# A three-stage kernel on one core: the short key step moved inside its chunk, the second sample's low-rank sums moved beside the channel mixer

## The chip, the cores and the metric

The program runs on one core of a Trainium2 chip. Its engines work side by side, each through a list of its own in program order: TensorE (PE) multiplies, and its weight loads (PEld) overlap the products; VectorE (DVE) and ScalarE (ACT) work element by element; GpSimd (POOL) does little here but issue DMAs; SyncE (SP) issues most DMAs. Semaphores order work between engines. The metric is the device time of one execution in microseconds (us).

## The reference

Batch 2, sequence S = 3136, width 256, key width 64. Three stages, each fed by the one before, in fp32:

```
attention:  a = max(z z^T / S, 0)^2            scores S x S, key width 64
            x = u * (a v)
layer 1:    h = (x^T U) V  (rank 32 over the sequence);  y = x + h^T
            out1 = y + max(y w1a, 0) w2a       256 -> 1024 -> 256
layer 2:    m = real(fft2(out1));  y = out1 + m
            n = (y - mean) / sqrt(var + 1e-6)  over the width
            out2 = y + max(n w1b, 0) w2b
```

## The kernel before

All large products use numbers split into a high part (rounded to the matmul's format, fp32r) and a low part (the rest); a product is high x high + high x low + low x high. The split costs one cast and one subtraction an operand (`hcopy` on ACT, `sub` on DVE, lines 92 to 96; profile rows with L93 and L96 are all of these).

*Attention* (lines 380 to 691). Per sample there are 7 chunks of 448 queries, 14 in all. A chunk runs over 13 key steps `p`: steps 0 to 11 take 256 keys. The key width of 64 fills half of the array's rows, so its two halves hold two blocks of keys, and two matmuls run side by side as a pair. `scores` (line 521) issues 6 matmuls (3 pairs), then ACT takes max and square (L541, L544), and DVE casts (L545) and subtracts. `values` and `products` (lines 552 to 587) multiply with the values into four PSUM banks, two per half `a` of the width: 12 pairs for a full step. Step 12 holds only the 64 keys that are left: 3 half-wide score pairs and 3 product pairs. It is the last of its chunk; the `a = 1` half of step 11 is put behind the `a = 0` half of step 12. Then `gate` (line 589) adds the two banks of each half and multiplies by u on DVE and stores the result to DRAM (`aT_d`) on SP. The scores run two steps ahead of the products (`LAG = 2`); at the last step of a chunk (`turn`) they come after the gate instead of before the products. PSUM has two double banks for scores and the four for sums.

Beside the steps, `ahead` and the main loop issue loads and splits: keys (`load_z`, `split_z`), queries, values (`load_v`, `split_v`; those of the second sample in chunk 6), and `conversions`: 41 generators that turn U, V and the four weight matrices from 64-bit words into high and low parts, one started every second step from step 9 on, at most two at once, each advanced once a step but for the last two steps of a chunk.

*Passage and layer 1.* When the attention's pools are closed, new ones take their memory: `mp` for working tiles, `xpool` for the attention's result, three pools for the eight PSUM banks. For each sample `mixer` (line 726) transposes 25 token tiles of 128, casts, and sums them with U into one bank, two tiles behind; `misc()` gives the transposes one of three banks in turn. For the first sample, 12 tiles come from four early loads into the common pool's P tiles, the rest from four large loads of `xT`. `finish_G` copies the sums, multiplies with a replicating matrix and splits. Then the second sample's mixer runs two tiles at a time, in turn with the first sample's `finish_G` and the first chunk's `prep1`; only when both are through, the 28 chunks of the channel mixer begin (14 of layer 1, 14 of layer 2; lines 993 to 1017), 8 steps each: `hidden` (6 matmuls), then `project` of the step before the last (6 matmuls). Generators in `active` advance once a step beside them: the next chunk's preparation, the second layer's Fourier transform (`fourier`, whose `features` ends in four DVE operations and eight additions), and its weights.

What sets the order is the program order on each engine, written out by hand by these loops. The parts that the change touches are `Weights.split` (181), `finish_G` (210), `load_z` (393), `split_v` (449), `scores` (521), `products` to `gate` (552 to 596), the loop over `steps` (598 to 691), the pools (703 to 724), `mixer` (726), `features` (867), `weights` (950) and the opening (979 to 992).

## Time and profile before

| | |
|---|---|
| median of 3 runs | 1207.67 us (1206.24 to 1208.36) |
| profiled execution, its own time | 1207.86 us |
| its span, first to last instruction | 1206.1 us |
| mean granted TensorE clock | 0.992 |
| instructions | 21307 |
| DMA moved | 69.39 MB, 58 GB/s over the span |

The time of an execution is a little longer than its span. In the rows further down, a line of a timeline is: start and length in us, engine, source line, operation, tiles written <- read, shapes, count, and in brackets how long the engine was idle before and what ended that. 9 in PE's slices of the page means 90% or more:

```profile
## 2 busy tenths in 40 slices
PE   8999999999999999997899999999999999999998
PEld 7899999898999999996799998999998888999997
DVE  7878887899778666565544646475676788767674
ACT  7877777887777666663422324333255444444442
POOL 0001000000000000000000000110000110000000
PEclk9999999999999999998999999999999999999999
```

Attention fills slices 1 to 18, layer 1 about 20 to 29.

### The profile page before, as it was taken

What the parts mean: (1) busy time and instruction counts of PE and PEld (TensorE: products, weight loads), DVE (VectorE), ACT (ScalarE), POOL (GpSimd) and SP (SyncE); (2) the same over time, 40 slices, a digit from 0 to 9 for tenths busy, and PEclk for the clock granted to TensorE, in tenths of its full rate; (3) what the DMA queues carried; (4) which work ended last, traced back from release to release, by engine and by line L of the source; (5) the groups of instructions that cost most, each with busy time, mean ns of one, the idle gap of its engine ahead of it and who ended that gap; (6) DMA issues with size and microseconds to landing.
All of it is one profiled execution on the core that took longest, in us unless ns stands there. A gap on an engine that the chain in (4) does not pass through costs nothing.

```text
span 1206.1 us, 21307 instructions
## 1 busy us (share of the span) xinstructions
PE 1180.0 (98%) x8488; PEld 1080.5 (90%) x8488; DVE 831.5 (69%) x1581; ACT 662.6 (55%) x1102; POOL 52.7 (4%) x104
## 2 busy tenths in 40 slices
PE   8999999999999999997899999999999999999998
PEld 7899999898999999996799998999998888999997
DVE  7878887899778666565544646475676788767674
ACT  7877777887777666663422324333255444444442
POOL 0001000000000000000000000110000110000000
PEclk9999999999999999998999999999999999999999
DMA  4303322243212111017000101211012111111111
GB/s 133 103 17 88 89 65 71 58 139 118 81 51 92 44 40 39 1 45 282 8 16 17 29 9 61 60 26 33 8 49 81 49 45 28 39 31 39 32 39 46
DMA packets 58691, 69.39 MB, mean 58 GB/s; under 512 B 11294, under 2 KB 52672, under 8 KB 58592
## 3 DMA queue, kind: packets, MB, share of 16 engines
q1 hardware_dynamic: 52896, 60.72, 15.9%
q0 software_dynamic: 5696, 7.31, 3.0%
q8 instruction: 67, 1.10, 0.4%
q14 instruction: 32, 0.26, 0.1%
HBM read 47.96 MB, written 19.96 MB: 56 GB/s over the span
## 4 chain that ended last, share of the span: by engine, by line
PE 82%; DVE 9%; ACT 4%; DMA 3%; issue 2%; SPq 0%; DVEq 0%; ACTq 0%
PE psO L567 29%; PE psH L324 7%; PE psH L326 7%; PE psH L325 7%; PE psC L350 7%; PE psC L349 7%; PE psC L351 7%; PE psS L535 7%; PE psC L733 1%; DMA vraw<-in_v 1%; ACT P L544 1%; DVE Hl L330 1%; ACT P L541 1%; DVE h L545 1%; DVE Vt L96 1%
## 5 line engine op out<-in xcount | busy, mean ns | idle before, releaser
L567 PE MATMUL psO<-h,Vt 64*128 64x448 f32 x2744 | 434.7, 366 | 2.2 <-DVE aT L594 1.5
L567 PEld LDWEIGHTS psO<-h,Vt 64*128 64x128 f32 x2744 | 279.2, 185 | 24.6 <-DVE aT L594 4.9
L567 PE MATMUL psO<-l,Vt 64*128 64x448 f32 x1372 | 274.5, 368 | 1.3 <-DVE l L96 1.3
L330 DVE SCALAR_TENSOR_TENSOR Hl<-psH,Hh 128x448 fp32r<-128x448 f32 x224 | 138.9, 622 | 157.0 <-ACT Hh L329 155.8
L96 DVE TENSOR_TENSOR l<-P,h 128x896 fp32r<-128x896 f32 (+2 forms) x211 | 209.9, 995 | 24.0 <-ACT h L93 17.7
L329 ACT ACTIVATE Hh<-psH 128x448 fp32r<-128x448 f32 x224 | 120.9, 542 | 180.5 <-PE psH L326 179.4
L541 ACT ACTIVATE P<-psS 128x896 f32<-128x896 f32 (+1 forms) x183 | 161.3, 882 | 96.2 <-PE psS L535 94.8
L545 DVE CAST h<-P 128x896 fp32r<-128x896 f32 (+1 forms) x183 | 110.5, 604 | 106.6 <-ACT P L544 106.0
L544 ACT ACTIVATE P<-P 128x896 f32<-128x896 f32 (+1 forms) x183 | 168.5, 922 | 5.8
L324 PE MATMUL psH<-h,w 128*128 128x448 f32 x448 | 167.7, 374 | 0.0
L349 PE MATMUL psC<-Hh,w 128*128 128x448 f32 x448 | 163.7, 365 | 1.4 <-DVE P L372 1.4
L350 PE MATMUL psC<-Hl,w 128*128 128x448 f32 x448 | 163.7, 365 | 0.9 <-DVE Hl L330 0.9
L326 PE MATMUL psH<-h,w 128*128 128x448 f32 x448 | 164.2, 366 | 0.0
L325 PE MATMUL psH<-l,w 128*128 128x448 f32 x448 | 164.0, 366 | 0.0
L351 PE MATMUL psC<-Hh,w 128*128 128x448 f32 x448 | 163.0, 364 | 0.0
L567 PEld LDWEIGHTS psO<-l,Vt 64*128 64x128 f32 x1372 | 143.0, 185 | 13.8 <-DVE l L96 3.8
L535 PE MATMUL psS<-Q,KT 64*128 64x448 f32 x1002 | 130.5, 363 | 2.2 <-ACT KT L93 1.9
L535 PEld LDWEIGHTS psS<-Q,KT 64*128 64x128 f32 x1002 | 99.0, 185 | 8.7 <-ACT KT L93 2.4
L349 PEld LDWEIGHTS psC<-Hh,w 128*128 128x128 f32 x448 | 84.0, 188 | 9.5 <-issue 1.9
L350 PEld LDWEIGHTS psC<-Hl,w 128*128 128x128 f32 x448 | 84.1, 188 | 9.1 <-DVE Hl L330 2.1
L324 PEld LDWEIGHTS psH<-h,w 128*128 128x128 f32 x448 | 84.3, 188 | 7.6
L326 PEld LDWEIGHTS psH<-h,w 128*128 128x128 f32 x448 | 84.1, 188 | 7.5
(282 smaller groups left out, 1159.4 us busy)
## 6 DMA issues: line engine op xcount, KB each, us to landing
uT<-in_uT SPq DMA_DIRECT2D x14, 448.0 KB, 4.4
aTd<-aT SPq DMA_DIRECT2D x14, 448.0 KB, 2.9
vraw<-in_v SPq DMA_DIRECT2D x24, 256.0 KB, 2.8
out<-P SPq DMA_DIRECT2D x27, 224.0 KB, 2.0
scr<-wst SPq DMA_DIRECT2D x16, 256.0 KB, 2.0
xT<-aTd SPq DMA_DIRECT2D x2, 1600.0 KB, 8.4
Vs<-Vd POOLq DMA_DIRECT2D x28, 112.0 KB, 2.5
rs<-rsd POOLq DMA_DIRECT2D x14, 224.0 KB, 3.6
```

The source lines that it names most:

```text
L96: tt(out=o, in0=a, in1=b, op=ALU.subtract)
L324: mm(ps[:, 0:CH], wh, self.h[:, a], start=a == 0, stop=False)
L325: mm(ps[:, 0:CH], wh, self.l[:, a], start=False, stop=False)
L326: mm(ps[:, 0:CH], wl, self.h[:, a], start=False, stop=a == 1)
L330: stt(out=l, in0=ps[:, 0:CH], scalar=0.0, in1=f(h), op0=ALU.max, op1=ALU.subtract)
L349: mm(dst, wh, h, start=k == 0, stop=False)
L350: mm(dst, wh, l, start=False, stop=False)
L351: mm(dst, wl, h, start=False, stop=k == 7)
L535: mm(ps[:, j, 0:w], k, q[r, kq, o : o + w], start=(kk, kq) == (0, 0), stop=kq == 1)
L541: act(out=dst, in_=ps[:, j : j + m, 0:w], func=AF.Relu, scale=1.0 / S)
L544: act(out=A[:, x], in_=A[:, x], func=AF.Square)
L567: mm(o[fa][i][:, 0:CH], vt[r, j, k, fa * 128 : fa * 128 + 128], x[r, j * CH : j * CH + CH], start=p == 0 and n == 0, stop=p == 12 and (a = ...
```

## The change

- The order of key steps becomes 0 to 5, 12, 6 to 11: the short step is the seventh of its chunk, the gate comes after step 11, and the held-back half is that of step 10. Key loads follow the new order.
- `scores` multiplies high x high, then key high x query low, then key low x query high.
- At the start, the first keys are loaded from ACT's queue, the first value tile is cast on DVE, and the first scores are issued ahead of the loop.
- Conversions start every third step instead of every second, from step 13 on, and none in the first sample's first and last chunk.
- The last chunk's gate works in a P tile of the common pool and stores on POOL's queue; three early loads (9 tiles) follow instead of four.
- The PSUM pools of the mixer stage are opened in another order; `xT` comes in seven pieces in the order of use.
- The first sample's 25 tiles run alone; then `finish_G` and the first chunk's preparation run beside 12 tiles of the second sample; its other 13 tiles, one a step, and its `finish_G` run beside the channel mixer's first steps. `finish_G` yields twice, and the clearing of its tile comes first.
- A yield splits `features` after its four DVE operations, and the cast and subtraction of the second layer's weights fall into two steps; one more buffer for them.

```diff
@@ -180,6 +180,10 @@
...
+            for _ in self.parts(k, y):
+                pass
+
+        def parts(self, k, y):
             part, q = divmod(k, 2)
...
@@ -190,6 +194,7 @@
...
             hcopy(dst[:, 0], y)
+            yield
             sub(dst[:, 1], y, f(dst[:, 0]))
...
@@ -208,8 +213,8 @@
     def finish_G(b, g, P):
-        nc.vector.memset(P[64:128], 0.0)
         nc.vector.tensor_copy(P[0:64], g[0:64, 0:D])
+        yield
         yield
...
@@ -396,7 +401,8 @@
...
                     src = zT[b, :, i * 768 : i * 768 + 768].rearrange("d (p j n) -> d j p n", j=2, n=128)
-                    load(out=raw[r], in_=src[:, j])
+                    dma = nc.scalar.dma_start if (b, i) == (0, 0) else load
+                    dma(out=raw[r], in_=src[:, j])
                 else:
...
@@ -449,7 +455,7 @@
...
             t = Vt[b, p] = big.tile([128, 2, 2, D], F32R, tag="V", name="Vt", bufs=13)
-            hcopy(t[:, 0:n, 0, :], raw[:, 0:n, :])
+            (nc.vector.tensor_copy if (b, p) == (0, 0) else hcopy)(t[:, 0:n, 0, :], raw[:, 0:n, :])
             sub(t[:, 0:n, 1, :], raw[:, 0:n, :], f(t[:, 0:n, 0, :]))
@@ -523,7 +529,7 @@
...
             w = CH if p < 12 else CH // 2
-            for kk, kq in ((0, 0), (1, 0), (0, 1)):
+            for kk, kq in ((0, 0), (0, 1), (1, 0)):
                 for j, r in enumerate(halves):
...
@@ -532,7 +538,7 @@
...
                     o = j * w if p == 12 else 0
-                    mm(ps[:, j, 0:w], k, q[r, kq, o : o + w], start=(kk, kq) == (0, 0), stop=kq == 1)
+                    mm(ps[:, j, 0:w], k, q[r, kq, o : o + w], start=(kk, kq) == (0, 0), stop=kk == 1)
             A, h, l = ptile(), ctile("h", F32R), ctile("l", F32R)
...
@@ -569,7 +575,7 @@
...
                         start=p == 0 and n == 0,
-                        stop=p == 12 and (a == 1 or n + i == 1),
+                        stop=p == 11 and n == len(todo) - 1,
                     )
...
@@ -579,23 +585,26 @@
...
-            if p == 12:
-                products(b, qc, 11, 1)
-                del prob[b, qc, 11]
-            if p != 11:
+            if p == 11:
+                products(b, qc, 10, 1)
+                del prob[b, qc, 10]
+            if p != 10:
                 products(b, qc, p, 1)
...
         def gate(b, qc):
-            t = att.tile([128, 2, CH], F32, tag="aT", name="aT")
+            last = (b, qc) == (1, NC - 1)
+            t = c2(ptile()) if last else att.tile([128, 2, CH], F32, tag="aT", name="aT")
             o, u = acc.pop((b, qc)), uq.pop((b, qc))
...
             tt(out=t, in0=t, in1=u, op=ALU.mult)
-            load(out=aT_d[b][:, :, qc * CH : qc * CH + CH].rearrange("a p n -> p a n"), in_=t)
-
-        steps = [(b, qc, p) for b in range(NB) for qc in range(NC) for p in range(NP)]
+            (late_dma if last else load)(out=aT_d[b][:, :, qc * CH : qc * CH + CH].rearrange("a p n -> p a n"), in_=t)
+
+
+        order = [*range(6), 12, *range(6, 12)]
+        steps = [(b, qc, p) for b in range(NB) for qc in range(NC) for p in order]
         LAG = 2
...
@@ -613,25 +622,29 @@
...
         load_v(0, 1)
+        load_z(0, 1)
         split_q(0, 0)
-        load_z(0, 1)
         split_v(0, 0)
         split_z(0, 0)
-        started, converting = [0], []
+        scores(0, 0, 0)
+        started, converting = [10], []
...
                 b, qc, p = steps[i]
-                scores(b, qc, p)
+                if i:
+                    scores(b, qc, p)
+                p = i % NP
                 if qc == 0 and b == 0:
...
                         if p < 6:
-                            load_z(0, 2 + p // 2)
-                        split_z(0, 1 + p // 2)
+                            load_z(0, (4, 2, 3)[p // 2])
+                        split_z(0, (1, 4, 2, 3)[p // 2])
                     if p > 0:
-                        split_v(0, p)
+                        split_v(0, order[p])
                     if p + 2 < NP:
-                        load_v(0, p + 2)
+                        load_v(0, order[p + 2])
                 if p == 2:
...
@@ -642,7 +655,8 @@
...
                     active.append(constants())
-                if i >= 9 and i - started[-1] >= 2 and len([g for g in active if g in converting]) < 2:
+                quiet = (b, qc) not in ((0, 0), (0, NC - 1))
+                if quiet and i - started[-1] >= 3 and len([g for g in active if g in converting]) < 2:
                     job = next(jobs, None)
...
@@ -655,7 +669,7 @@
...
         for i in range(-LAG, len(steps)):
-            turn = i >= 0 and steps[i][2] == NP - 1
+            turn = i >= 0 and steps[i][2] == 11
             if not turn:
...
@@ -664,23 +678,24 @@
...
                     ahead(i + LAG)
+                n = i % NP
                 if b == 0 and qc == NC - 1:
                     load_v(1, p)
-                    if p > 0:
-                        split_v(1, p - 1)
+                    if n > 0:
+                        split_v(1, order[n - 1])
                 if (b, qc, p) == (1, 0, 0):
-                    split_v(1, NP - 1)
+                    split_v(1, 11)
                 if (b, qc) == (1, NC - 1):
...
                         chunks[0].load()
-                    if p == NP - 2:
-
-                        for k in range(4):
+                    if p == 11:
+
+                        for k in range(3):
                             t = ptile().rearrange("p (a n) -> p a n", a=2)[:, :, 0:384]
...
                 for g in list(active):
-                    if p >= NP - 2 and (b, qc) != (1, NC - 1):
+                    if n >= NP - 2 and (b, qc) != (1, NC - 1):
                         break
...
@@ -700,10 +715,10 @@
...
     xpool = ctx.enter_context(tc.tile_pool(name="xpool", bufs=1))
-    psH = late["psH"] = ctx.enter_context(tc.tile_pool(name="psH", bufs=3, space=PSUM))
     psX = ctx.enter_context(tc.tile_pool(name="psX", bufs=1, space=PSUM))
     psC = late["psC"] = ctx.enter_context(tc.tile_pool(name="psC", bufs=1, space=PSUM))
-    misc_pools.extend((psX, t) for t in "mxg")
+    psH = late["psH"] = ctx.enter_context(tc.tile_pool(name="psH", bufs=3, space=PSUM))
+    misc_pools.extend([(psX, "m"), (psX, "x"), (psC, "C1")])
...
@@ -719,13 +734,15 @@
...
-    for b in range(NB):
-        for s in (slice(1536, S), slice(0, 1536)):
-            load(out=xT[b][:, :, s], in_=aT_d[b][:, :, s].rearrange("a p n -> p a n"))
+    def load_x(b, s, e):
+        load(out=xT[b][:, :, s:e], in_=aT_d[b][:, :, s:e].rearrange("a p n -> p a n"))
...
-        g = psC.tile([128, 512], F32, tag=f"C{b}", name=f"psC{b}")
+        pool, tag = ((psC, "C0"), (psX, "g"))[b]
+        g = pool.tile([128, 512], F32, tag=tag, name="ps_" + tag)
+        P = mp.tile([128, 512], F32, tag="wst", name="wst")[:, 0:D]
+        nc.vector.memset(P[64:128], 0.0)
...
@@ -737,7 +754,7 @@
...
             for a in range(2):
-                if b == 0 and k < 12:
+                if b == 0 and k < 9:
                     t = early[k // 3][:, a, k % 3 * 128 : k % 3 * 128 + 128]
...
@@ -750,12 +767,11 @@
...
                 sums(*ready.pop(0))
-            if k % 2:
-                yield
+            yield
         while ready:
...
         yield
-        yield from finish_G(b, g, mp.tile([128, 512], F32, tag="wst", name="wst")[:, 0:D])
+        yield from finish_G(b, g, P)
...
@@ -888,6 +904,7 @@
...
             end = first + n // 64
+            yield
...
@@ -948,10 +965,10 @@
...
     def weights(i):
-        ts = {}
+        ts, halfway = {}, []
         for k in range(12):
             if k < 8:
-                ts[k] = mp.tile([128, 256], F32, tag="wraw", name="wraw", bufs=3)
+                ts[k] = mp.tile([128, 256], F32, tag="wraw", name="wraw", bufs=4)
                 load(out=ts[k], in_=wb_d[i][k])
...
@@ -963,9 +980,12 @@
...
                     sub(y[:, a], y[:, a], ps[:, 0:128])
-                wb[i].split(k - 2, ts.pop(k - 2))
-            elif 1 < k < 10:
-                wb[i].split(k - 2, ts.pop(k - 2))
+            for p in list(halfway):
+                next(p, None)
+                halfway.remove(p)
+            if 1 < k < 10:
+                halfway.append(wb[i].parts(k - 2, ts.pop(k - 2)))
+                next(halfway[-1])
             yield
...
@@ -976,20 +996,24 @@
...
+        for b, s, e in (
+            (0, 1152, 1792), (0, 1792, 2464), (0, 2464, S), (0, 0, CH), (1, 0, 1568), (0, CH, 1152), (1, 1568, S),
+        ):
+            load_x(b, s, e)
+        mix0, mix1 = mixer(0), mixer(1)
+        for _ in range(26):
+            next(mix0)
+
         def first():
-            yield
-            yield from last_G
+            yield from mix0
+            yield
             yield from chunks[0].prep()
-        mix0, mix1 = mixer(0), mixer(1)
-        for _ in range(13):
-            next(mix0)
-        last_G = mix0
-        opening = [mix1, first()]
-        while opening:
-            for g in list(opening):
-                if next(g, "end") == "end":
-                    opening.remove(g)
+        for _ in first():
+            next(mix1)
+            next(mix1)
+        misc_pools.pop()
+        active.append(mix1)
         for i in range(nstep + 2):
...
@@ -1015,6 +1039,8 @@
...
                     active.remove(g)
+                    if g is mix1:
+                        misc_pools.append((psX, "g"))
```

## Rows read from the trace of the kernel before

**Rows 1.** Page, busy us (share of the span) and instructions of each engine.

```profile
PE 1180.0 (98%) x8488; PEld 1080.5 (90%) x8488; DVE 831.5 (69%) x1581; ACT 662.6 (55%) x1102; POOL 52.7 (4%) x104
```

**Rows 2.** PE's wait list: waiter <- releaser: total us, times, longest us.

```profile
PE psC L733 <- ACT nh L93: 7.1, 2, 6.7
...
PE psO L567 <- DVE aT L594: 1.5, 2, 1.2
...
PE psC L349 <- DVE P L372: 1.4, 1, 1.4
```

**Rows 3.** Windows: length, busy us (instructions) per engine, PEclk, DMA share, GB/s.

```profile
551.83:562.07 10.24, 3.69 (x17) 3.42 (x17) 2.12 (x6) 2.04 (x6) 1.14 (x4) 0.51 1.01 401
...
582.55:585.97 3.42, 3.11 (x15) 3.11 (x16) 1.82 (x6) 1.20 (x4) 0.00 (x0) 0.54 0.00 0
```

**Rows 4.** Timeline of PE, score matmuls: start, us, line, operation, tiles, count, [idle before].

```profile
45.45 0.77 PE L535 MATMUL psS<-Q,KT 64*128 64x448 f32 x6
...
317.49 0.37 PE L535 MATMUL psS<-Q,KT 64*128 64x448 f32 x2
...
508.11 0.58 PE L535 MATMUL psS<-Q,KT 64*128 64x448 f32 x4
...
540.36 0.77 PE L535 MATMUL psS<-Q,KT 64*128 64x448 f32 x6
...
543.42 0.49 PE L535 MATMUL psS<-Q,KTl 64*128 64x224 f32 x6
```

**Rows 5.** Timeline, end of attention and first sums of the mixer.

```profile
549.11 0.36 PE L567 MATMUL psO<-h,Vt 64*128 64x448 f32 x1
...
550.73 1.09 DVE L595 TENSOR_TENSOR aT<-aT,uT 128x896 f32<-128x896 f32 x1
...
557.95 0.37 ACT L93 CAST nh<-ps_m 128x256 fp32r<-128x256 f32 x1 [7.91 <-DMA aTd<-aT]
...
558.38 0.47 PE L733 MATMUL psC<-nh,Uhl 128*64 128x256 f32 x1 [6.73 <-ACT nh L93]
```

**Rows 6.** Timeline, second sample's sums and the channel mixer's first matmul.

```profile
575.91 0.45 PE L215 MATMUL ps_x<-wst,repc 128*128 128x256 f32 x1 [0.57 <-DVE wst L212]
...
579.59 1.02 POOL L230 DMA_DIRECT2D Vs<-Vd  x2 [20.46 <-PE ps_x L244]
...
580.92 0.38 PE L744 MATMUL ps_m<-ident,xT 128*128 128x128 f32 x2
...
581.38 0.38 PE L744 MATMUL ps_x<-ident,xT 128*128 128x128 f32 x2
...
581.85 0.62 DVE L96 TENSOR_TENSOR l<-P,h 128x448 fp32r<-128x448 f32 x1 [0.63 <-ACT h L93]
...
592.30 0.55 PE L324 MATMUL psH<-h,w 128*128 128x448 f32 x1
```

**Rows 7.** Timeline, the start.

```profile
6.96 0.62 ACT L93 CAST Vt<-vraw 128x512 fp32r<-128x512 f32 x1 [2.54 <-DMA vraw<-in_v]
...
8.05 0.47 PE L535 MATMUL psS<-Q,KT 64*128 64x448 f32 x2 [1.85 <-ACT KT L93]
...
8.83 1.80 PE L535 MATMUL psS<-Q,KT 64*128 64x448 f32 x10 [0.31 <-DVE KT L96]
...
10.43 0.58 PE L567 MATMUL psO<-h,Vt 64*128 64x448 f32 x2
```

**Rows 8.** Timeline of DVE at the turn of a chunk.

```profile
164.56 1.09 DVE L96 TENSOR_TENSOR l<-P,h 128x896 fp32r<-128x896 f32 x1
...
165.56 0.62 DVE L594 TENSOR_TENSOR aT<-psO,aT 128x448 f32<-128x448 f32 x1
```

**Rows 9.** Page, costliest groups: count, busy us, mean ns, idle before.

```profile
L541 ACT ACTIVATE P<-psS 128x896 f32<-128x896 f32 (+1 forms) x183 | 161.3, 882 | 96.2 <-PE psS L535 94.8
...
L545 DVE CAST h<-P 128x896 fp32r<-128x896 f32 (+1 forms) x183 | 110.5, 604 | 106.6 <-ACT P L544 106.0
...
L544 ACT ACTIVATE P<-P 128x896 f32<-128x896 f32 (+1 forms) x183 | 168.5, 922 | 5.8
```

## The prediction

> **What bounds the kernel now.** I read the page's busy line first, then PE's wait list, then the timeline at each place that the list names, then windows with the granted clock. PE is busy for 98% of the span [rows 1], so removing busy time of another engine is worth nothing by itself; only PE's idle time, its waits too short to be listed, and its time at the lower clock can go. The wait list has one large entry: 7.1 us on PE for the first sums of the low-rank product [rows 2]. The rest is small: 1.5 us for the gate that ends an attention chunk, 1.4 us for a chunk's end in the second layer [rows 2]. The windows add to the passage from attention to the channel mixer two stretches, 10.24 and 3.42 us long, in which the granted clock is about 0.5, the 1.2 GHz level [rows 3].
>
> Attention hides a loss that the list does not show. A full step is 15 pairs of 448-column matmuls (3 of scores, 12 of products; the two of a pair run side by side on 64 rows each); two score starts in a row lie 543.42 - 540.36 = 3.06 us apart [rows 4], 0.204 us a pair. A chunk is 12 such steps (180 pairs), the short step's 3 product pairs, and its 3 score pairs at half width (some 0.11 each): 183 x 0.204 + 0.33 = 37.7 us. The undisturbed chunks take (508.11 - 317.49) / 5 = 38.12 us [rows 4], so 0.4 us is lost in each. All twelve from 45.45 to 508.11 take 462.66 [rows 4], 5.2 us more than 12 x 38.12: those are the chunks that also convert weights and split the second sample's values.
>
> **The change, part by part.** The sum is made against the profiled execution, 1207.86 us (span 1206.1); it stands 0.2 us above the median of 1207.67.
>
> *The first wait of the mixer.* PE's last attention product starts at 549.11; the gate's product on DVE ends at 550.73 + 1.09 = 551.82; but ACT's first cast of the mixer comes at 557.95, ended by the landing of the gate's own store [rows 5]. The cast writes memory that the attention's pools held, and the store was still reading from there. The change puts the last gate's tile into the common pool and its store on POOL's queue, so the last reader of the old memory is the DVE product. Then the cast can start at 551.85 and the first sums 558.38 - 557.95 = 0.43 us behind it, at 552.3 instead of 558.38: 6.1 us. Least: 0, if another transfer still holds that memory. Most: 6.1 plus half of the 3.69 us that PE worked at the lower clock until 562.07 [rows 3], 7.9. I take 6.1, since PE still idles some 2 us there. Late next is the data: the first sums take nine token tiles from three early loads, which no longer stand behind the gate's store on SP. The tenth needs 640 columns, 0.66 MB. At the 401 GB/s of the first stretch [rows 3] that is 1.6 us from the attention's end, about 549.5; the pieces ahead of the second sample, 2432 columns, and its own 1568 take 10.2 us, until about 560 and some us for the landing, and the second sample cannot start before 552.3 + 25 x 0.46 = 563.8. SP's later pieces wait for the store, as now; they have that slack.
>
> *The second sample's sums.* Now its 25 tiles run before the first channel-mixer matmul at 592.30 [rows 6]. Afterwards 12 run there, beside the first sample's finish and the first chunk's preparation, as they do now, and 13 go one a step beside the mixer's chunks. The twelfth tile's transposes start at 580.92, the thirteenth's at 581.38 [rows 6]: one tile costs PE 0.46 us. From 581.38 on, the mixer could start; its fifth matmul, 0.8 us in, needs the last low half of the preparation, which ends at 581.85 + 0.62 = 582.47, so it waits 0.3. It starts at 581.7 instead of 592.30: 10.6 us. The finish's wait of 0.57 at 575.91 [rows 6] gets two yields of cover: 11.2. Against that stand 13 x 0.46 = 6.0 and the second finish's matmul, 0.6: 4.6 net. The moved casts and subtractions hide beside the mixer's matmuls, since ACT and DVE are idle 45% and 31% of the span [rows 1]; the first chunks then share two banks for transposes and the next preparation. If the mixer opens at the lower clock, as the old stretch had it for 3.42 us [rows 3], half of that, 1.7, comes off: 2.9. I take 4.0; ends 1.5 (the lower clock and three 0.46 us waits for those banks) and 5.5.
>
> *The start.* PE's first products start at 10.43; before them it waits 1.85 us for a key cast that stands behind the value cast of 6.96 on ACT, then until 8.83 for DVE's low half [rows 7]. The value cast goes to DVE, the key's loads to ACT's queue, and the pair order lets the low key half come last. Then PE is bounded by the query (unchanged) and by DVE's value and key halves, about 7.2 instead of 8.83: 1.6 us, and 0.3 for the conversions that leave chunk 0: 1.9. No DMA issued by ACT is in this trace; POOL's pair took 1.02 [rows 6], and so much may stand before ACT's query casts: least -1.0. Most 3.6, if the clock does not fall.
>
> *Short step at mid-chunk.* At the turn now, DVE starts a 1.09 us subtraction at 164.56 and only behind it, at 165.56, the gate's two additions, each of which frees two banks for the next chunk's products [rows 8]. With a full step last, 12 pairs (2.4 us) instead of 7 (1.4) lie between the end of the first two banks' sums and the next scores, and the subtraction that stood in the way belongs to scores that are then 24 pairs old instead of 15: DVE reaches the additions in time. 13 turns lose 0.4; I leave 0.1: gain 4.0. In mid-chunk the scores before and after the short step's products come 1.2 us apart instead of 3.06, while ACT's two passes take 0.88 + 0.92 and DVE's 0.60 + 1.09 [rows 8, 9]. For the earlier of the two, the short step's products, the later scores, a full step and one more set of scores, 3 + 3 + 12 + 3 = 21 pairs or 4.3 us, lie ahead of its own products, against 3.5 us on ACT and DVE: cover of some 0.6 with the hand-overs. I charge 0.1 x 14 = 1.4. Ends for turns and mid-chunk together: +5 and -14 (a wait of 1.0 in each chunk).
>
> *Conversions every third step, none in chunks 0 and 6.* They spread into the second sample's chunks, the undisturbed ones, where ACT and DVE leave over 1.2 us of a 3.06 us step free. Of the 5.2 us above I take 3.2; ends 0 and 5.2.
>
> *Second layer.* A yield behind four DVE operations of the features and halves of the weight split a step apart: of the 1.4 us [rows 2] I take 0.8; ends -1.4 (the moved additions meet another chunk's end) and 1.4. The fourth weight buffer, the banks' new order and the earlier clearing of a tile cost nothing of their own: the first transposes may start earlier, but the cast behind them does not.
>
> Sum: 6.1 + 4.0 + 1.9 + 4.0 - 1.4 + 3.2 + 0.8 = 18.6. 1207.86 - 18.6 = 1189.3.
>
> **A rule that speaks against it.** POOL's pair of loads was issued in 1.02 us while DVE worked beside it [rows 6], so no stretching is seen. The Trainium skill ("SBUF — State Buffer", "SBUF: two separate sides") says that POOL's descriptors can't be written while DVE runs certain copies between SBUF tiles, and that such a DMA is starved. No run here shows that for a store.
>
> **Rivals.**
> 1. *The forecast, 1189*: 55%.
> 2. *Only the passage gains.* The stalls of the turn move to mid-chunk: turns and mid-chunk 0, conversions 1.0, second layer 0: 1207.86 - (10.1 + 1.9 + 1.0) = 1195. For it: DVE is busy 69% of the span [rows 1], so little is left where three kinds of work meet. Against: the lag. 22%.
> 3. *More than forecast.* The clock stays up through the passage and the start (1.8 + 1.7), and half of the 4.7 us that I left at turns, mid-chunk and conversions goes too: 1207.86 - 18.6 - 3.5 - 2.3 = 1183. Against: some 2 us of idle PE stay in the passage. 12%.
> 4. *The store on POOL comes late.* SP's loads of the second sample stand behind it, and its tiles hold up PE, which works in order. It costs nothing until the store lands some 5 us behind 551.8, then 1 us for each us; at the 6.1 us more of today's store, 1195. This is what the rule above would do. 6%.
> 5. *Slower.* The short step breaks the pipeline in mid-chunk: after it, products wait on DVE in every chunk as the worst turn does now, 1.2 us of the 1.5 [rows 2], 14 x 1.2 = 16.8, with nothing gained at turns or from conversions: 1207.86 - 10.1 + 16.8 = 1214.6 with a start that gains nothing. It is slower from 10.1 / 14 = 0.7 us a chunk. Against: the 0.6 us of cover. 5%.
>
> **Numbers.** The likeliest is 1189. Rivals 1 and 3 and most of 2 and 4 lie in 1182 to 1198, its ends being the full clock with all stalls gone and rival 2 with the lower end of the second sample's part. 0.2% (2.4 us) is what a measurement tells from no change: faster 0.93, same 0.02 (between 4 and 5), slower 0.05.
>
> **What would show it.** The wait on the first sums down from 7.1 to about 1; attention's last product near 549.1 - 7.7 = 541.4 (start, turns, conversions); the first mixer matmul near 592.30 - 17.3 - 7.7 = 567; a chunk pitch of 37.8 instead of 38.12; scores after the short step without waits on ACT or DVE. Wrong if the first cast still waits for a DMA, if PE waits on DVE's l in each chunk, or if token transposes of the second sample wait for xT.

## The result and the profile after

The changed kernel takes 1194.44 us (median of 4 runs, 1192.73 to 1195.27) against 1208.01 for the kernel before (4 runs, 1206.24 to 1208.53): a ratio of 0.9888, 95% interval 0.9871 to 0.9906. That is 13.6 us gained, where 18.6 were forecast. The profiled execution took 1195.08 us, 12.78 less than that of before; its span is 1193.3 us.

In the trace after, L541 is the scores, L547 and L550 ACT's two passes, L551 DVE's cast, L573 the products, L601 to L603 the gate and its store, L738 the loads of xT, L750 and L761 the sums and transposes of the low-rank product, L329 to L331 the channel mixer's first layer. The page's busy line, against [rows 1]:

```profile
PE 1176.6 (99%) x8488; PEld 1089.3 (91%) x8488; DVE 833.3 (70%) x1582; ACT 663.0 (56%) x1101; POOL 54.1 (5%) x105
```

PE's wait list (waiter <- releaser: total us, times, longest), against [rows 2]:

```profile
PE psO L573 <- DVE l L96: 2.0, 4, 0.7
PE psO L573 <- DVE h L551: 1.5, 2, 0.9
...
PE ps_C L750 <- ACT nh L93: 1.1, 1, 1.1
```

The 7.1 us for the first sums are 1.1, as forecast. The gate's 1.5 us are gone. New are 3.5 us in which attention's products wait for the two halves of the scores. To see where, I cut both traces at the start of the weight load of each chunk's first product and of the mixer's first matmul, and at the fourth mixer chunk:

| stage, us | before | after | gained |
|---|---|---|---|
| until the first product | 10.06 | 8.23 | 1.83 |
| attention chunk 0 | 40.58 | 43.38 | -2.80 |
| chunks 1 to 4 | 153.33 | 152.00 | 1.33 |
| chunk 5 | 39.56 | 40.84 | -1.28 |
| chunks 6 and 7 | 78.66 | 75.97 | 2.69 |
| chunks 8 to 12 | 190.62 | 190.00 | 0.62 |
| chunk 13, to its last product | 36.10 | 36.15 | -0.05 |
| last attention product to first mixer matmul | 43.37 | 25.79 | 17.58 |
| mixer chunks 0 to 2 of the first layer | 58.19 | 65.29 | -7.10 |
| second layer, 13 of its chunks | 282.04 | 282.09 | -0.05 |

The rest of the span differs by less than 0.1 us. The sum of the gains is 12.77.

The timeline of the passage after, against [rows 5] and [rows 6] (start, us, engine, line, operation, [idle before <- releaser]):

```profile
546.77 0.37 PE L573 MATMUL psO<-h,Vt 64*128 64x448 f32 x2
...
548.39 1.09 DVE L602 TENSOR_TENSOR P<-P,uT 128x896 f32<-128x896 f32 x1
...
549.57 0.37 ACT L93 CAST nh<-ps_m 128x256 fp32r<-128x256 f32 x1 [1.86 <-DVE P L602]
...
549.79 0.74 POOL L603 DMA_DIRECT2D aTd<-P  x1 [403.79 <-DVE P L602]
...
549.99 0.33 PE L750 MATMUL ps_C<-nh,Uhl 128*64 128x256 f32 x1 [1.14 <-ACT nh L93]
...
572.48 0.36 PE L329 MATMUL psH<-h,w 128*128 128x448 f32 x1
```

The first cast is now ended by the gate's product on DVE, not by a DMA. From the last attention product to the first sums it takes 549.99 - 546.77 = 3.22 us instead of 558.38 - 549.11 = 9.27. From there to the mixer it takes 22.49 us instead of 592.30 - 558.38 = 33.92. Windows of the clock, and of the first three mixer chunks (length, busy us of PE, PEld, DVE, ACT, POOL, PEclk, DMA share, GB/s), against [rows 3]:

```profile
35.69:39.10 3.41, 3.41 (x21) 3.02 (x20) 3.27 (x6) 2.65 (x4) 0.00 (x0) 0.50 0.29 79
551.10:554.51 3.41, 3.41 (x19) 3.41 (x18) 1.70 (x4) 1.66 (x5) 0.59 (x2) 0.50 1.01 351
572.48:637.77 65.29, 65.11 (x345) 59.07 (x344) 31.81 (x59) 22.21 (x47) 3.08 (x6) 1.00 0.05 13
```

The passage has one stretch at the 1.2 GHz level instead of two, and there is a new one in chunk 0. In the third window PE is busy for 65.11 of 65.29 us: the tiles cost their own PE time there and nothing in waits.

### The profile page after: what moved, and what is told of

It reads as the page before. It is cut to its first block, busy times and chain, and to the rows that moved or that the text cites. A ratio compares the mean times of both kernels' runs of the same rounds, so it can differ in the third digit from the quotient of the medians.

```text
span 1193.3 us, 21313 instructions
## 1 busy us (share of the span) xinstructions
PE 1176.6 (99%) x8488; PEld 1089.3 (91%) x8488; DVE 833.3 (70%) x1582; ACT 663.0 (56%) x1101; POOL 54.1 (5%) x105
## 4 chain that ended last, share of the span: by engine, by line
PE 87%; DVE 4%; issue 4%; ACT 2%; DMA 1%; POOL 0%; SPq 0%; ACTq 0%; DVEq 0%; POOLq 0%
PE psO L573 34%; PE psS L541 8%; PE psH L329 7%; PE psH L330 7%; PE psH L331 7%; PE psC L354 7%; PE psC L355 7%; PE psC L356 7%; DMA zraw<-in_zT 1%; PE ps_C L750 1%; DVE Hl L335 1%; ACT P L547 0%; ACT P L550 0%; PE ps_g L750 0%; PE ps_x L761 0%
## 5 line engine op out<-in xcount | busy, mean ns | idle before, releaser
L573 PE MATMUL psO<-h,Vt 64*128 64x448 f32 x2744 | 432.9, 365 | 1.7 <-DVE h L551 1.5
L573 PEld LDWEIGHTS psO<-h,Vt 64*128 64x128 f32 x2744 | 276.5, 185 | 14.2 <-DVE h L551 1.3
L573 PE MATMUL psO<-l,Vt 64*128 64x448 f32 x1372 | 268.8, 368 | 2.1 <-DVE l L96 2.0
L547 ACT ACTIVATE P<-psS 128x896 f32<-128x896 f32 (+1 forms) x183 | 161.4, 882 | 59.0 <-PE psS L541 57.0
L551 DVE CAST h<-P 128x896 fp32r<-128x896 f32 (+1 forms) x183 | 110.6, 605 | 87.9 <-ACT P L550 86.5
L550 ACT ACTIVATE P<-P 128x896 f32<-128x896 f32 (+1 forms) x183 | 168.6, 922 | 5.7
L329 PE MATMUL psH<-h,w 128*128 128x448 f32 x448 | 167.7, 374 | 0.0
L331 PE MATMUL psH<-h,w 128*128 128x448 f32 x448 | 164.1, 366 | 0.0
L573 PEld LDWEIGHTS psO<-l,Vt 64*128 64x128 f32 x1372 | 140.4, 185 | 13.4 <-DVE l L96 8.0
L541 PE MATMUL psS<-Q,KT 64*128 64x448 f32 x1002 | 129.4, 363 | 0.7 <-ACT P L547 0.3
L541 PEld LDWEIGHTS psS<-Q,KT 64*128 64x128 f32 x1002 | 99.4, 185 | 5.3 <-ACT P L547 0.7
L331 PEld LDWEIGHTS psH<-h,w 128*128 128x128 f32 x448 | 84.1, 188 | 7.4
L329 PEld LDWEIGHTS psH<-h,w 128*128 128x128 f32 x448 | 84.3, 188 | 7.3
```

The source lines that it names most:

```text
L329: mm(ps[:, 0:CH], wh, self.h[:, a], start=a == 0, stop=False)
L331: mm(ps[:, 0:CH], wl, self.h[:, a], start=False, stop=a == 1)
L541: mm(ps[:, j, 0:w], k, q[r, kq, o : o + w], start=(kk, kq) == (0, 0), stop=kk == 1)
L547: act(out=dst, in_=ps[:, j : j + m, 0:w], func=AF.Relu, scale=1.0 / S)
L550: act(out=A[:, x], in_=A[:, x], func=AF.Square)
L573: mm(o[fa][i][:, 0:CH], vt[r, j, k, fa * 128 : fa * 128 + 128], x[r, j * CH : j * CH + CH], start=p == 0 and n == 0, stop=p == 11 and n == ...
```

## The experiments

Each changes the changed kernel ("after") and was timed beside the kernel before.

**1. Chunk 0: a third yield between the loads and the casts of the constants.** In chunk 0, ACT's list after (first fence) and PE's (second):

```profile
30.17 0.30 ACT L93 CAST fA<-P 128x128 fp32r<-128x128 f32 x1 [2.59 <-DMA P<-in_fd]
...
30.88 0.91 ACT L547 ACTIVATE P<-psS 128x896 f32<-128x896 f32 x1
```

```profile
31.84 0.87 PE L541 MATMUL psS<-Q,KT 64*128 64x448 f32 x6 [0.34 <-ACT P L547]
33.58 0.47 PE L573 MATMUL psO<-h,Vt 64*128 64x448 f32 x2 [0.87 <-DVE h L551]
34.62 0.47 PE L573 MATMUL psO<-l,Vt 64*128 64x448 f32 x2 [0.56 <-DVE l L96]
```

ACT stands at a constant that has not landed, and the scores' pass queues behind it. PE then waits three times, 1.77 us in all, and from 35.69 on runs at the lower clock for 3.41 us, half of which is lost.

```diff
         yield
         yield
+        yield
```

> One yield more before the casts of the constants (three instead of two). Theory A: chunk 0 is long (43.4 us from its first products to those of chunk 1) because ACT, which works in order, stands 2.6 us at a constant that has not landed, right behind the short step, where few products are queued on PE; the stall of 1.8 us on PE then brings the lower clock for 3.4 us. With one more full step of cover ACT does not wait: chunk 0 takes 39.0 to 40.5 us, no lower clock near 35 us, total 3 to 4 us less than the changed kernel (about 1191). Rival B: after the earlier start chunk 0 is short of loaded values, or ACT and DVE can't keep pace with the splits: chunk 0 stays at 42.5 us or more.

Measured: 1191.23 us (1191.0 to 1193.46), ratio 0.9862 [0.9847, 0.9877]. No wait for a constant is left on ACT, and chunk 0 takes 40.88 instead of 43.38, a little above what theory A gave. In this execution the lower clock came at 7.63 and reached into chunk 0. Six kernels with an unedited chunk 0 take 41.50 to 44.33 there, so 40.88 lies below them all: the wait for the constant was a cause of the loss. Number 9 below, with the same edit, shows that it was not the only one. Of the difference between the two profiled executions, 1.4 us stand not here but in the passage (last section).

**2. Chunk 5: no conversions there.** PE after, in chunk 5, has these idle times:

```profile
217.02 0.47 PE L573 MATMUL psO<-l,Vt 64*128 64x448 f32 x2 [0.61 <-DVE l L96]
...
225.12 0.47 PE L573 MATMUL psO<-h,Vt 64*128 64x448 f32 x2 [0.66 <-DVE h L551]
...
226.25 0.47 PE L573 MATMUL psO<-l,Vt 64*128 64x448 f32 x2 [0.65 <-DVE l L96]
```

```diff
-                quiet = (b, qc) not in ((0, 0), (0, NC - 1))
+                quiet = (b, qc) not in ((0, 0), (0, NC - 2), (0, NC - 1))
```

> No conversions start in chunk 5, where the second sample's keys are loaded and split. Theory A: chunk 5 (40.84 us in the changed kernel, 38.00 without a disturbance) is long because conversions and key splits meet at the short step on DVE and ACT: it falls to 38.0 to 38.5, total 2.5 us less (about 1192). Rival B: ACT stands at a key cast whose load has not landed (2.7 us in its wait list), whatever else is queued: chunk 5 stays above 39.8.

Measured: 1192.48 us (1190.24 to 1193.93), ratio 0.9866 [0.985, 0.9882]. Chunk 5 takes 38.34 instead of 40.84, and PE has no listed wait in it. The key loads and splits of the second sample stayed, so they alone do no harm. Nor do conversions alone: in the changed kernel chunk 4 (first line) holds as many of them as chunk 5 (second line) and takes 37.97. These are windows of the conversions' tile `stg` only: length, busy us of DVE, ACT and POOL, clock, DMA share, GB/s.

```profile
165.64:203.61 37.97, 8.03 (x24) 5.17 (x12) 0.00 (x0) 1.00 0.21 65
203.61:244.45 40.84, 8.02 (x24) 5.17 (x12) 0.00 (x0) 1.00 0.25 71
```

It is both together that the chunk has no room for.

**3. The short step last again, all else as after.**

```diff
-        order = [*range(6), 12, *range(6, 12)]
+        order = [*range(13)]
...
-            turn = i >= 0 and steps[i][2] == 11
+            turn = i >= 0 and steps[i][2] == 12
```

The held-back half and the order of the key loads go back with it.

> The short step is put back to the end of its chunk, with its held-back half; all else as in the changed kernel. Theory A: the move brings 0.12 us in each undisturbed chunk and costs more than that in chunks 0 and 5, where waits fall behind the short step: undisturbed chunks 38.1 us, chunk 0 near 40.5, chunk 5 near 39.5, attention ends 1.5 to 3 us earlier than in the changed kernel (last product at 546.6). Rival B, the one on record: the move is worth about 0.3 us a chunk and the long chunks have other causes: undisturbed chunks 38.1 to 38.3, chunks 0 and 5 as long as now, attention ends 1.5 us later or more.

Measured: 1191.97 us (1191.38 to 1192.63), ratio 0.9865 [0.9849, 0.9882]. This is the run that splits attention's sum. From first to last product:

| us | before | short step last | after |
|---|---|---|---|
| chunk 0 | 40.58 | 40.28 | 43.38 |
| chunk 5 | 39.56 | 39.19 | 40.84 |
| chunk 7 | 39.44 | 39.02 | 38.00 |
| undisturbed, each | 38.12 | 38.12 | 38.00 |
| all 14 chunks | 538.85 | 535.88 | 538.35 |

By one profile of each, all that is new in attention but the moved step gains 538.85 - 535.88 = 2.97, 2.66 of it in chunks 1 to 7; I take it as that of the conversions' new times. The moved step then costs 538.35 - 535.88 = 2.47: it gains 0.12 in an undisturbed chunk and 1.0 in chunk 7, and loses 3.10 in chunk 0 (some 1.7 of it the clock) and 1.65 in chunk 5. In this kernel ACT waits even longer for the same constant, but PE (second fence) waits once, and the granted clock does not fall behind it:

```profile
31.21 0.30 ACT L93 CAST fA<-P 128x128 fp32r<-128x128 f32 x1 [2.92 <-DMA P<-in_fd]
```

```profile
35.66 0.47 PE L573 MATMUL psO<-l,Vt 64*128 64x448 f32 x2 [0.57 <-DVE l L96]
```

So the same wait of 2.6 to 2.9 us on ACT costs 0.57 us of PE's time where full steps follow it, and 1.77 where the short step is near, with a stretch at the lower clock behind it in some profiles (last section).

Chunk 0 compares less cleanly than the table looks, because the clock at the start differs. Before, a stretch at a granted clock of 0.50 reaches 2.7 us into it:

```profile
9.36:12.77 3.41, 3.41 (x22) 3.01 (x20) 3.12 (x7) 3.38 (x6) 0.00 (x0) 0.50 0.46 134
```

With the short step last, the first product pairs start 0.37 us apart, as in that stretch, until about 10.7, 2.0 us into the chunk, and 0.20 apart later; the clock column gives 1.00 here, so this is read from the pairs alone:

```profile
9.08 0.57 PE L573 MATMUL psO<-h,Vt 64*128 64x448 f32 x2
9.45 0.63 PE L573 MATMUL psO<-l,Vt 64*128 64x448 f32 x2
```

In the changed kernel neither is there. Half of 2.7 and of 2.0 us are an estimate of what this cost the first two columns, 1.4 and 1.0. So the 0.30 gained in chunk 0 can be the clock alone, and the moved step may have cost some 1 us more there than 3.10.

**4. All of the second sample's tiles ahead of the mixer.**

```diff
-        misc_pools.pop()
-        active.append(mix1)
+        run(mix1)
+        misc_pools[-1] = (psX, "g")
```

> The second sample's last 13 tiles and its finish run ahead of the first channel-mixer step again, none beside it; all else as in the changed kernel. Theory A, the step on record: alone a tile costs 0.49 us and waits, beside the mixer 0.46 us: the first mixer matmul comes 9 to 11 us later relative to the end of attention (25.8 us in the changed kernel), the first three mixer chunks are 6.5 to 7.1 us shorter in sum, total 3 to 4 us more (about 1198). Rival B: the tiles cost PE the same time in either place, and the passage gained by the first wait alone: total within 1 us of the changed kernel.

Measured: 1197.23 us (1195.82 to 1198.12), ratio 0.9906 [0.9892, 0.9921]. The first sums and the first mixer matmul:

```profile
550.56 0.33 PE L750 MATMUL ps_C<-nh,Uhl 128*64 128x256 f32 x1 [1.14 <-ACT nh L93]
...
582.49 0.55 PE L329 MATMUL psH<-h,w 128*128 128x448 f32 x1
```

The mixer starts 9.53 us later after the last attention product than in the changed kernel, and its first three chunks take 58.19 again, 7.10 less. Moving the 13 tiles is worth 9.53 - 7.10 = 2.43, less than expected. From first sums to mixer it takes 582.49 - 550.56 = 31.93 without the move, against 33.92 before it: 1.99 of the passage's gain needs no moved tile. The kernel before has two stretches at the lower clock there [rows 3], this one has one of 3.4 us.

**5. The last gate's store on SP again, its tile still in the common pool.**

```diff
-            (late_dma if last else load)(out=aT_d
+            load(out=aT_d
```

> The last gate's store goes back to SP's queue, ahead of the seven loads of xT; its tile stays in the common pool. Theory A: what held the first cast of the mixer was the memory of the gate's tile, not the queue: the first sums start at the same distance from the last attention product as in the changed kernel (3.2 to 3.6 us), total within 1 us of it. Rival B: the queue did it: the first sums start 3 us or more later.

Measured: 1202.1 us (1200.66 to 1202.67), ratio 0.9957 [0.9942, 0.9972]. SP and PE:

```profile
548.19 0.36 SPq L603 DMA_DIRECT2D aTd<-P  x1
...
548.64 2.05 SPq L695 DMA_DIRECT2D P<-aTd  x3
...
554.29 0.66 PE L761 MATMUL ps_m<-ident,P 128*128 128x128 f32 x2 [8.47 <-DMA P<-aTd]
```

The three early loads stand behind the store in SP's list, and the store waits for the gate's product. PE then waits 8.47 us for tokens that in the changed kernel were long there. So rival B of the expectation held, not theory A.

**6. The last gate's tile in the attention's pool again, its store on POOL.**

```diff
-            t = c2(ptile()) if last else att.tile([128, 2, CH], F32, tag="aT", name="aT")
+            t = att.tile([128, 2, CH], F32, tag="aT", name="aT")
```

> The last gate works in a tile of the attention's pool again; its store stays on POOL's queue. Theory A: the first cast waits for that store to land: the first sums start 8 to 10 us behind the last attention product instead of 3.2, the lower clock lasts longer than 3.4 us, total 5 to 7 us more (1199 to 1202). Rival B: the loads in order of use and the banks brought the gain: first sums within 1 us of the changed kernel.

Measured: 1202.75 us (1201.66 to 1203.07), ratio 0.9963 [0.9948, 0.9977].

```profile
548.10 0.74 POOL L603 DMA_DIRECT2D aTd<-aT  x1 [403.64 <-DVE aT L602]
...
556.00 0.18 POOL L730 MEMSET raw<- 128x98 f32 x1 [7.16 <-DMA aTd<-aT]
556.04 0.37 ACT L93 CAST nh<-ps_m 128x256 fp32r<-128x256 f32 x1 [10.02 <-DMA xT<-aTd]
...
556.46 0.48 PE L750 MATMUL ps_C<-nh,Uhl 128*64 128x256 f32 x1 [9.29 <-ACT nh L93]
```

The cast waits for the landing of the store, as before the change (POOL's own memory clearing, released at the same time, names it). Each half of the edit alone leaves PE waiting 8 to 9 us; only both together take the wait away.

**7. The second layer's edits undone** (the yield behind the features, and the weights split at once).

```diff
             end = first + n // 64
-            yield
...
-                halfway.append(wb[i].parts(k - 2, ts.pop(k - 2)))
-                next(halfway[-1])
+                wb[i].split(k - 2, ts.pop(k - 2))
```

> The yield in the features and the halves of the weight split are undone. Theory A: the two edits only move DVE's work and the waits with it: the fourteen second-layer chunks (282.04 before, 282.09 changed, first to last start) take 281.8 to 282.4. Rival B, the one on record: they are worth 0.8 us: 282.7 or more.

Measured: 1193.61 us (1193.25 to 1194.16), ratio 0.9888 [0.9871, 0.9904], the changed kernel's own ratio. The 13 chunks take 282.02 with the edits undone and 282.09 with them: they are worth nothing.

**8. The turn: the next scores between the held-back half and the last six product pairs.** At a turn of the changed kernel, DVE (first fence) and PE (second) show

```profile
394.31 0.62 DVE L601 TENSOR_TENSOR aT<-psO,aT 128x448 f32<-128x448 f32 x1
396.17 0.62 DVE L601 TENSOR_TENSOR aT<-psO,aT 128x448 f32<-128x448 f32 x1 [1.24 <-ACT aT L93]
...
398.84 1.09 DVE L96 TENSOR_TENSOR l<-P,h 128x896 fp32r<-128x896 f32 x1
```

```profile
399.69 0.39 PE L573 MATMUL psO<-h,Vt 64*128 64x448 f32 x2
399.99 0.47 PE L573 MATMUL psO<-l,Vt 64*128 64x448 f32 x2
400.29 0.57 PE L573 MATMUL psO<-h,Vt 64*128 64x448 f32 x4
400.71 0.36 PE L573 MATMUL psO<-l,Vt 64*128 64x448 f32 x2
```

The gate's additions no longer hold up PE, but its second half and the low part of the next chunk's second step follow one another on DVE. That low part ends at 398.84 + 1.09 = 399.93, and PE's pair starts behind it. The four pairs from 399.69 to 400.71 take 1.02 us instead of 4 x 0.204 = 0.82: 0.2 lost.

```diff
...
+                between()
             if p != 10:
                 products(b, qc, p, 1)
...
-                values(b, qc, p)
+                values(b, qc, p, lambda: ahead(i + LAG))
                 if turn:
                     gate(b, qc)
-                    ahead(i + LAG)
```

> New: at the turn of a chunk the next scores go between the held-back half and the last 6 pairs of products instead of behind them. Theory A: what an undisturbed chunk still loses (38.00 us against 37.7 of products and scores) is one wait for the low part of the second step, whose scores come late at the turn; 1.2 us earlier they are in time: 37.7 to 37.8 a chunk, total 2.5 to 3.5 us less (about 1191). Rival B: ACT then takes the next step's squares ahead of the gate's second copy, and the next products wait for their banks: 38.0 or more a chunk.

Measured: 1235.97 us (1233.29 to 1236.73), ratio 1.0235 [1.0217, 1.0254]; the chunks from 1 on take 40.5 to 43.4 us. PE's wait list:

```profile
PE psO L573 <- DVE aT L602: 18.7, 13, 1.5
PE psO L573 <- ACT aT L93: 7.8, 13, 1.0
```

The scores that stand behind the gate are what hides it. Issued ahead of it they leave the next chunk's products waiting for the banks, 26.5 / 13 = 2.0 us a turn, and six more stretches at the lower clock follow inside attention, behind the one in chunk 0.

**9 and 10. Put together.** Number 9 joins the edits of 1 and 2. Number 10 has the quiet chunk 5 and starts the constants a chunk later, the conversions with them:

```diff
-        started, converting = [10], []
+        started, converting = [13], []
...
-                if (b, qc, p) == (0, 0, 5):
+                if (b, qc, p) == (0, 1, 0):
```

> The third yield of the constants and the conversion-free chunk 5 together. If the two long chunks have separate causes, their gains add: chunk 0 39.2 to 40.9 us, chunk 5 38.3 to 38.4, the other chunks 38.0; 4.5 to 6 us less than the changed kernel, about 1189 and below either alone. If they share a cause, the sum is that of one alone, about 1191.5.

> The constants are loaded and cast at the start of chunk 1, where few loads are under way, instead of in chunk 0; the conversions start at step 16; chunk 5 free of conversions. If chunk 0 is long because its five small loads stand in SP's queue ahead of the values and ACT waits for either, chunk 0 falls to 38.5 to 39.3 us and chunk 1 stays at 38.0 to 38.3: 1 to 2 us less than with the third yield, about 1187.5. If what is left of chunk 0 is the splits of its keys and values, chunk 0 stays at 39.5 us or more and nothing is gained against the third yield.

Measured: number 9 1189.96 us (1188.58 to 1190.79), ratio 0.9855 [0.9842, 0.9869]; number 10 1189.26 us (1188.39 to 1189.87), ratio 0.985 [0.9836, 0.9863]. Both beat both kernels; between the two the runs do not decide, and the 1 to 2 us that number 10 was to gain on the third yield are not seen. In number 10 chunk 0 takes 38.83, chunk 5 38.83, the last attention product starts at 541.36, where the prediction had 541.4, and the first mixer matmul at 567.03, where it had 567. The gains left out were in the main those of chunks 0 and 5. That the numbers meet so closely is partly chance: the undisturbed chunks still take 38.0 us, not the 37.8 that was forecast. In its first 52 us PE has one wait left in the list, that of the start:

```profile
PE psS L623 <- DVE warm L615: 1.3, 1, 1.3
```

In number 9 chunk 5 takes 38.27, but chunk 0 still 42.57: values that land late and a stretch at the lower clock at 38.16. With the constants in chunk 0, it stays the chunk that differs most from run to run: 41.50 to 44.33 in the six kernels whose chunk 0 is that of the changed kernel.

## Why the prediction was right in its direction and 5 us off in its size

The time lies in the range, 5 us above the forecast, and next to rival 2's 1195. Rival 2 is not what happened, though: the conversions gained almost what the forecast took, and the moved step lost. That its number is so near is chance. Term by term, against the profiled execution:

| term | taken | measured | from |
|---|---|---|---|
| first wait of the mixer | 6.1 | 6.05 | 9.27 - 3.22 |
| second sample's sums | 4.0 | 2.43 | experiment 4 |
| lower clock and rest of the passage | 0 | 1.99 | experiment 4 |
| start | 1.9 | 1.83 | first product |
| turns and mid-chunk | 4.0 - 1.4 = 2.6 | -2.47 | experiment 3 |
| conversions (chunk 0: the clock too) | 3.2 | 2.97 | experiment 3 |
| second layer | 0.8 | -0.05 | experiment 7 |
| sum | 18.6 | 12.75 | |

**The step that failed is "Short step at mid-chunk".** It was wrong in two ways. At the turn it took 0.3 of the 0.4 us a chunk loses; 38.12 became 38.00, so 0.12. The additions do come early enough, but I stopped there, and did not follow DVE on to the low part behind them. In mid-chunk it charged each of 14 chunks 0.1 us against a cover worked out as 0.6. All chunks but 0 and 5 show no wait there at all, those that convert weights among them, so that cover holds beside the scores and a conversion. In chunks 0 and 5 there is more: a cast that waits 2.59 us for a constant, or conversions on top of the second sample's key splits. There the loss was 3.10 + 1.65 = 4.75 us, most of the 5.07 between 2.6 and -2.47. The trace of before held both places, and the prediction named the cover but did not ask where else ACT waits for a DMA. The end of -14 that it kept, a wait of 1.0 in each chunk, had the right kind of event and the wrong number of chunks.

**The passage** came out as forecast, 17.58 - 7.10 = 10.48 against 10.1, but its parts stand in other proportions, so the close sum is partly luck: the second sample brought less than was taken, and 1.99 came that was put at nothing. The first wait fell by what was worked out. Experiments 5 and 6 show that both causes named for it were needed: the memory that the store was reading, and the early loads behind the store on SP. The second sample's term took the whole of 592.30 - 581.7 as the tiles' doing. Some of it was time at the 1.2 GHz level: PE's busy 3.69 and 3.11 us of [rows 3] lose half, 3.4, and the 3.41 us after lose 1.7. That difference of 1.7 would be most of the 1.99 that came without the move. On the other side the tiles cost the mixer 7.10, not 6.6.

**Start and conversions** came out near what was taken. The start's 1.83 is that of one execution: in the ten other kernels with the same start the first product comes at 8.24 to 8.71 instead of 8.23, a gain of 1.35 or more. In the changed kernel it is more than lost again in chunk 0, for the reason above. One reading behind the conversions was wrong: the prediction took the chunks from 317.49 to 508.11 as free of them, but in the trace of before chunks 8 and 9 also convert, as do 3 and 4, and all four take 38.1 us. Behind chunk 0, what exceeds that stands in chunks 1 and 2 (38.42 and 38.66) and in 5 to 7, beside the second sample's splits. **The second layer's** 1.4 us of [rows 2] are gone from the list, but 13 chunks take as long as before with the edits and without them; why the wait that left the list freed no time was not followed up.

**Rival 4** did not occur. SP waits for the landing of the store, and issues the last piece of xT behind it:

```profile
SPq L738 <- DMA aTd<-P: 6.4, 1, 6.4
```

The transfer itself, in the list of DMA issues (KB, us from issue to landing):

```profile
aTd<-P POOLq DMA_DIRECT2D x1, 448.0 KB, 7.3
```

It lands at 549.79 + 7.3 = 557.1, 7.6 us behind the gate's product and past the 5 us from which the prediction had it cost something; still PE has no listed wait for xT, so the slack was larger. Before, from SP's queue, the landing came 557.95 - 551.82 = 6.1 us behind the product; what the 1.5 us between the two are stays open, and they held up nothing. The Trainium skill ("SBUF — State Buffer", "SBUF: two separate sides") says that POOL's descriptors can't be written while DVE runs certain copies between SBUF tiles. This run does not test it: from the store's issue, which took 0.74 us, to its landing DVE ran no copy, only a clearing of memory until 549.87 and the subtractions of the tiles' low halves, which read PSUM. **Rival 3** had the clock stay up through the passage and the start: in the passage one of two stretches is gone, and the one from 9.36 on is gone from the start, but chunk 0 has a new one. **Rival 5** had the short step break every chunk by 0.7 us or more: it broke two of 14. Experiment 8, a kernel slower by that kind of wait, is what such a trace looks like: 13 equal entries in PE's list.

## What to carry to other kernels

A step that moves takes its cover with it: work out the cover in the worst chunk, with every DMA wait of the engines that feed PE, and not in the undisturbed one. Before crediting a stall to a move, find the next late operation behind it on the same engine. Where a transfer holds both memory and a place in a queue, change both: either half alone left PE waiting at least as long as before (8.47 and 9.29 us against 6.73).

## What was not expected of the hardware

In chunk 0, waits of 0.34, 0.87 and 0.56 us with PE at work between them were followed by 3.41 us at a granted clock of 0.50, the 1.2 GHz level, which cost as much again as the waits themselves (1.7 against 1.77 us). But such waits do not decide it. Five experiments keep this chunk 0 unedited and have waits at the same place: in 2 and 4, of 1.43 and 2.69 us in sum, a stretch follows; in 5, 6 and 7, of 1.66, 1.43 and 2.15 us, none does. In experiment 7, PE's waits (first fence) and the window behind them (second, granted clock 1.00):

```profile
32.71 0.88 PE L541 MATMUL psS<-Q,KT 64*128 64x448 f32 x6 [0.73 <-ACT P L547]
34.45 0.47 PE L573 MATMUL psO<-h,Vt 64*128 64x448 f32 x2 [0.86 <-DVE h L551]
35.49 0.47 PE L573 MATMUL psO<-l,Vt 64*128 64x448 f32 x2 [0.56 <-DVE l L96]
```

```profile
35.69:39.10 3.41, 3.28 (x32) 2.80 (x32) 3.31 (x6) 3.38 (x5) 0.00 (x0) 1.00 0.26 79
```

What decides it no run here shows. In the passage, the stretch of 3.4 us at 1.2 GHz is there in the profiles of the changed kernel and of experiments 2, 7, 8 and 10, and absent in those of 1, 3 and 9, with no edit that bears on the passage. From the last attention product to the mixer this makes 25.8 against 24.4 us: 1.4 us that no edit explains, and that are part of what experiments 1, 3 and 9 gained on the changed kernel in their profiles.
